# Sliding-window attention feeding a squared-ReLU MLP: the first two token blocks as one unit, w_in in five pieces, a new order

## The chip, the cores and the metric

The kernel runs on one core of a Trainium2 chip. The metric is device time in microseconds (us), the median of several executions. A core has TensorE (PE, matrix products; its weight loads are shown as PEld), VectorE (DVE), ScalarE (ACT), GpSimd (POOL) and SyncE (SP). Transfers are issued from the queues of POOL, SP and ACT, and 16 DMA engines carry them.

## The reference

```python
scores = scale * q @ k.T             # 8 batches, 8 heads, 576 positions, head size 64
bias = slopes * -abs(rel)            # ALiBi: one slope for each head
scores = where(0 <= rel < 128, scores + bias, -1e9)
attn = softmax(scores)               # in float32
x = (attn @ v) -> [4608, 512]        # heads side by side, tokens of all batches in a row
h = x @ w_in                         # [512, 2048]
g = maximum(h, 0) ** 2
out = g @ w_out                      # [2048, 512], float32
```

The window is 128 positions, so a block of 128 queries meets its own block of keys and the one before it.

## The kernel before, in words

**Tiling.** The 576 positions of a batch are four blocks of 128 and one of 64. There are 40 blocks, m = 0 to 39. The first eight are the first blocks of the eight batches (kind "diag", with no block before them); then come the other blocks, two batches at a time. The MLP works on nine groups g of 512 tokens.

**Attention of one block.** POOL loads k, q and v by DMA and casts them to bf16 (lines 408 and 413; block 0's k and q come over SP and ACT as float32, line 391, and DVE casts them). k and q are then transposed: for m < 8 on PE (`tp`, line 464, with copies `ev` by ACT or DVE), for the others by a DMA transpose from SP (`kqT`, line 450). Scores go into four PSUM banks with the tag "a" (`s`, line 520); ACT exponentiates them (`e`, line 544), DVE multiplies by a mask with bias and window in it (`m`, lines 552 to 559). PE multiplies by v in two halves of four heads (`pv`, line 587); v has a column of ones, which gives the sum. DVE takes the reciprocal (`r`, line 605) and normalises (`n`, line 609). The result is transposed into `xT`: on PE for m < 8 (`xp`, line 629, and a copy `x`), by a DMA transpose from SP for the others (`x`, line 617).

**MLP.** For groups 0 to 2 the first product is cut into units: `u g.r.e` (line 721) takes token range r and some of the 16 column blocks (fc) of w_in, always 512 columns of PSUM in a bank with the tag "h" (two of them). In group 0 a unit is 128 tokens by four fc, in groups 1 and 2 it is 256 tokens by two. From group 3 on, one step `fc g.fc` (line 739) takes 512 tokens by one fc. ACT applies ReLU (line 692), DVE squares into `g` (line 683). `o g.t.p` (line 766) multiplies quarter p of the 2048 values by w_out for token block t; after the fourth part ACT or DVE copies it out (`oe`) and SP stores it (`st`, line 790).

**What sets the order.** The kernel writes its own order. Every piece of work is a task with engines, an estimated length, dependencies, buffers and a key (a due time). `Plan.order` (lines 98 to 188) walks an estimated clock: on each engine it takes, of the tasks that can start within NEAR of the earliest, the one with the lowest key. LAND, `lat` and `dma` estimate when a transfer lands; LEAD says how far ahead of its first unit an attention block is due; the table ADJ shifts keys of single tasks by hand. On the chip these estimates only matter by the order that comes out of them; semaphores do the waiting. Where the plan sees a hole on PE in the first 30 us, `fill` (line 269) puts in matmuls on a tile of zeros that compute nothing. Eight more run at the start (line 434).

**Queues.** POOL's first transfers are set by the list FIRST: "b2" is block 2's k, q, v, "i1" a piece of w_in, "o1" a quarter of w_out. POOL keeps at most eight of its transfers under way: the ninth waits for the first to land. SP's queue is in order. Four buffers hold k and q (`kq`), nine hold v, three hold x. The transposes and stores that touch the prediction stand on SP as `st0.2.0 kqT10 st0.3.0 kqT11 x8 kqT12 x9 kqT13 kqT14 st1.0.0 x10`.

**Names in the change.** N_CUT is the number of first blocks whose transpose back (`xp`) is cut into two; N_PVH the number of first jobs whose `pv` uses an "h" bank instead of an "a" bank; N_HW the number of blocks loaded over SP and ACT. A unit waits for its piece of w_in (`t_win`) and for x of all its blocks (`t_x`).

Of the kernel before, what the change touches and what calls it, by code (L numbers as in the profile page):

```python
# [9 lines left out]
BF16 = mybir.dt.bfloat16  # L10
# [2 lines left out]

FIRST = ["b0", "b1", "b2", "i0", "i1", "o0", "i2", "b3", "i3", "o1", "o2", "o3", "b4", "b5", "b6", "b7"]
DIAG = [[0], [1], [2], [3], [4, 5], [6, 7]]
N_HW = 1
N_PE = 8
N_CUT = 2  # L20
N_PVH = 1
N_WARM = 8
FILL = 0.7
LEAD = 1160
IOTA = 3
TP, XP = "h", "h"
UNITS = {0: 128, 1: 256, 2: 256}
CUT = 384
SIZE = {"kq": 4, "v": 9, "kqT": 7, "P": 3, "x": 3}
DUE = {m: 200.0 * m - 1e5 for m in range(40)}  # L30

ADJ = {
    "e1.1": 9000135.6, "e19.2": -177.01, "e19.3": -468.76, "e2.1": 100084.3, "m2.0": 690.7, "m6.1": 98674.82,
    "mask0.6": 99479.82, "n6.1": 98853.62, "o0.1.2": -273.16, "o0.2.1": 39, "o0.3.2": -120.75, "o1.1.0": -108.3,
    "o1.2.3": -99095.7, "o1.3.1": -36.0, "o1.3.2": -98248.6, "o1.3.3": -224.85, "o2.0.0": -99746.7, "o2.0.1": -614.83,
    "o2.0.2": -99764.0, "o2.0.3": -321.48, "o2.2.1": -99007.0, "o2.3.0": -99983.4, "o2.3.1": -875.31,
    "pv0.1": 99179.79, "pv17.0": -148.06, "r0.1": 582.3, "reluu0.0.1": -99432.0, "reluu0.2.2": -9000091.1,
    "reluu0.2.3": -99589.6, "reluu1.0.0": -99692.3, "reluu2.1.2": -52.84, "s13": 168.43, "s17": -99446.52,
    "s20": 342.83, "squ0.1.0": 48, "squ0.2.3": 99864.0, "u0.1.0": -79.4, "u0.1.1": -99420.7, "u0.2.1": -99696.3,
    "u0.2.3": -98883.7, "u1.0.1": -98012.9, "u1.1.3": -99531.7, "u1.1.5": 191.7, "u1.1.6": -410.31,  # L40
    "u2.0.4": -100055.4, "u2.0.5": -342.1, "u2.0.6": -100078.7, "u2.0.7": -331.83, "u2.1.1": 78.7, "u2.1.2": 63.7,
    "u2.1.3": -99113.3, "u2.1.4": -79.4, "u2.1.7": -303.48,
}


def FUSED(g, u):
    return False


class Task:  # L50
# [20 lines left out]
class Plan:  # L71
# [2 lines left out]
    LAT = {"PE": 210.0, "ACT": 60.0, "DVE": 80.0, "POOL": 200.0, "SP": 200.0, "ACTQ": 200.0}  # L74
    BEGIN = {"POOL": 840.0, "SP": 740.0, "ACTQ": 740.0, "ACT": 2550.0, "DVE": 860.0, "PE": 1190.0}
    FIRST = {"POOL": 1100.0, "SP": 1150.0, "ACTQ": 1150.0}
    LAND = {"POOL": 1200.0, "SP": 2200.0, "ACTQ": 900.0}
    TO_SP = 600.0
    LANES = 8
    NEAR = {"PE": 60, "ACT": 0, "DVE": 25}  # L80
    FILL_UNTIL = 30000.0

    def __init__(self, bufs):
# [108 lines left out]
def kernel(  # L192
    ctx: ExitStack, tc: tile.TileContext, q, k, v, moe_w_in, moe_w_out, out
):
    nc = tc.nc
# [78 lines left out]
    def act(n):  # L274
        return n * 0.95 + 115.0
# [4 lines left out]
    def dve_p(n, rate=1):  # L280
        return n / rate / 0.96 + 185.0
# [65 lines left out]
    t_zero = plan.add({"DVE": 1300.0}, -1e5 + 950, zero, name="zero", later=25000.0)  # L347


    t_win = [None] * 4  # L350
    t_wout = [None] * 4

    def load_w(which, n, key):
        def emit():
            w = d_ff // 4
            if which == "in":
                nc.gpsimd.dma_start(w_in_sb[:, :, n * w:(n + 1) * w],  # L357
                                    moe_w_in[:, n * w:(n + 1) * w].rearrange("(c p) f -> p c f", p=128))
            else:
                nc.gpsimd.dma_start(w_out_sb[:, 4 * n:4 * n + 4, :],  # L360
                                    moe_w_out[n * w:(n + 1) * w, :].rearrange("(c p) f -> p c f", p=128))
        t = plan.add({"POOL": 780.0}, key, emit, dma=2600.0, name=f"w_{which}{n}")
        (t_win if which == "in" else t_wout)[n] = t

    s_kq, s_v, t_kq, t_v = {}, {}, {}, {}

# [7 lines left out]
    def load_block(m, key):  # L374
# [10 lines left out]
        if split:  # L385
            stage = stages[m]
            t_l = []
            for i, src in enumerate((k, q)):
                for r, (eng, e) in enumerate((("SP", nc.sync), ("ACTQ", nc.scalar))):
                    def fetch(i=i, src=src, r=r, e=e):  # L390
                        e.dma_start(view(stage, i)[:, r], source(src, m, split)[:, :, r])
                    t_l.append(plan.add({eng: 740.0}, key + 0.1 * i, fetch, dma=330.0, lat=1000.0,
                                        name=f"l{'kq'[i]}{m}.{r}"))

            def cast_kq(i):
                w = slice(i * d_model, (i + 1) * d_model)
                copy((c_k, c_q)[i],
                     kq[s_kq[m].idx][:, w].rearrange("s (i r d) -> s r i d", i=4, d=D),
                     stage[:, w].rearrange("s (r i d) -> s r i d", r=2, d=D))
            engs = {"DVE": 480.0, "ACT": 600.0} if m else {"DVE": 480.0}  # L400
            c_q = None
            c_k = plan.add(engs, key, lambda: cast_kq(0), t_l[0:2], [s_kq[m]], name=f"ck{m}")
            c_q = plan.add(engs, key, lambda: cast_kq(1), t_l[2:4] + [c_k], name=f"cq{m}")
            t_kq[m] = [c_k, c_q]
        else:
            def fetch_kq():
                for i, src in enumerate((k, q)):
                    nc.gpsimd.dma_start(view(kq[s_kq[m].idx], i), source(src, m, split))  # L408
            t_kq[m] = [plan.add({"POOL": 1780.0}, key, fetch_kq, [], [s_kq[m]], dma=2 * ns,
                                name=f"lkq{m}", count=2)]  # L410
# [229 lines left out]


    def ups(g):
        if UP[g] == 512:
            return [("fc", g, u) for u in range(16)]
        return [("unit", g, r, e) for r in range(512 // UP[g]) for e in range(16 * UP[g] // 512)]

    UP = {g: UNITS.get(g, 512) for g in range(NG)}
    work_list = ups(0)
    for g in range(NG):
        up = ups(g + 1) if g + 1 < NG else []  # L650
# [1 line left out]
            work_list += up[u:u + 1] + [("o", g, u // 4, u % 4)]  # L652

    def span_of(item):
        w = UP[item[1]]
        lo = item[1] * 512 + (item[2] * w if w < 512 else 0)
        return lo, lo + w

    def blocks(lo, hi):
        return [at[x] for r in range(lo // 128, hi // 128) for x in ranges[r]]  # L660
# [10 lines left out]

    g_slots, g_sq, g_first, o_slots = {}, {}, {}, {}

    def relu_square(g, slot, last_mm, key, out_of, fused):
        def square(a, b=None):
            if g_slots[g].tile is None:
                g_slots[g].tile = work.tile([128, FCB, 512], BF16, tag="g", bufs=2, name="g")
            o = out_of(g_slots[g].tile)
            i = a if len(o.shape) == 2 else a.rearrange("p (f t) -> p f t", f=o.shape[1])
            if fused:  # L680
                nc.vector.scalar_tensor_tensor(o, i, 0.0, i, op0=ALU.max, op1=ALU.mult)
            else:
                nc.vector.tensor_tensor(o, i, i, op=ALU.mult)  # L683
        if fused:
            ts = plan.add({"DVE": dve_p(512)}, key, lambda: square(slot.tile), [last_mm] + g_sq[g][:1], [], [slot],
                          name=f"rs{g}")
        else:
            srt = Slot("rt")

            def relu():  # L690
                srt.tile = work.tile([128, 512], BF16, tag="rt", bufs=3, name="rt")
                nc.scalar.activation(srt.tile, slot.tile, AF.Relu, bias=0.0, scale=1.0)  # L692
            tr = plan.add({"ACT": act(512)}, key, relu, [last_mm], [srt], [slot], name=f"relu{last_mm.name}")
            ts = plan.add({"DVE": dve(512, 2)}, key, lambda: square(srt.tile), [tr] + g_sq[g][:1], [], [srt],
                          name=f"sq{last_mm.name}")
        g_sq[g].append(ts)
        return ts

    def group(g):
        if g not in g_slots:  # L700
# [1 line left out]
            return [g_slots[g]]  # L702
        return []

    sq_of = {}

    def unit(g, r, e, key):

        new = group(g)
        slot = Slot("h")  # L710
        w = UP[g]
        nf = 512 // w
        lo = g * 512 + r * w
        ms = blocks(lo, lo + w)

        def emit():
            fill(t_mm, bank_of(slot, "h"))
            for f in range(nf):
                fc = nf * e + f
                for cc in range(C):  # L720
                    nc.tensor.matmul(slot.tile[:, f * w:(f + 1) * w], w_in_sb[:, cc, fc * 128:(fc + 1) * 128],  # L721
                                     xT[:, cc, lo:lo + w], start=cc == 0, stop=cc == C - 1)
        t_mm = plan.add({"PE": 4 * nf * mm(w)}, key, emit,
                        [t_win[nf * e // 4], g_first.get(g)] + [x for m in ms for x in t_x[m]], [slot] + new,
                        name=f"u{g}.{r}.{e}")
        g_first.setdefault(g, t_mm)
        ts = relu_square(g, slot, t_mm, key,
                         lambda gt: gt[:, nf * e:nf * e + nf, r * w:(r + 1) * w], FUSED(g, e + r))
        for t in range(r * w // 128, (r + 1) * w // 128):
            sq_of.setdefault((g, t, nf * e // 4), []).append(ts)  # L730

    def fc_step(g, fc, key):
# [3 lines left out]
        def emit():  # L736
            bank(slot, "h")
            for cc in range(C):
                nc.tensor.matmul(slot.tile, w_in_sb[:, cc, fc * 128:(fc + 1) * 128],  # L739
                                 xT[:, cc, g * 512:(g + 1) * 512], start=cc == 0, stop=cc == C - 1)  # L740
        t = plan.add({"PE": 4 * mm(512)}, key, emit,
                     [t_win[fc // 4], g_first.get(g)] + [x for m in blocks(g * 512, g * 512 + 512) for x in t_x[m]],
                     [slot] + new, name=f"fc{g}.{fc}")
        g_first.setdefault(g, t)
        ts = relu_square(g, slot, t, key, lambda gt: gt[:, fc, :], FUSED(g, fc))
        for r in range(4):
            sq_of.setdefault((g, r, fc // 4), []).append(ts)

# [84 lines left out]
```

## Time and profile before

| | |
|---|---|
| median of 3 runs | 316.77 us (316.46 to 316.91) |
| the profiled execution | 316.23 us |
| its span | 314.4 us |
| mean granted PE clock | 0.994 |
| PE busy | 306.3 us (97%), 2794 matmuls |
| DVE, ACT, POOL busy | 174.1, 170.7, 105.5 us |
| POOL's DMA queue: packets' time | 84.5% of 16 engines' span |
| fill and warm-up matmuls | 50 of 128 columns, 8 of 512 |

The span is the time from the first to the last instruction in the profile. Around it lie 1.83 us in that execution. Busy matmul times overlap each other slightly, so a group's busy time is more than what it takes on the path; the view of the chain gives the latter. The granted clock is the share of full speed at which PE was let run. "Idle before, releaser" names what ended a wait. A transfer's time to landing is counted from its issue.

### The profile page before, as it was taken

How to read it: one execution, taken by the hardware profiler on the slowest of the kernel's cores; microseconds unless marked ns; L12 is line 12 of the kernel's file. 1: busy time of each engine (PE TensorE's matmuls, PEld its weight loads, DVE VectorE, ACT ScalarE, POOL GpSimd, SP SyncE). 2: the span in 40 equal slices, each digit the busy share in tenths (PEclk: the TensorE clock that was granted, in tenths of full speed). 3: DMA queues.
4: the chain of work that ended last, by engine and by line, in shares of the span. 5: the costliest groups of instructions: out<-in, count | busy, mean ns of one | idle time of the engine just before them, and what ended most of it. 6: DMA issues, size and time to landing. Idle time of an engine off the chain costs nothing.

```text
span 314.4 us, 7113 instructions
## 1 busy us (share of the span) xinstructions
PE 306.3 (97%) x2794; PEld 176.0 (56%) x2794; DVE 174.1 (55%) x498; ACT 170.7 (54%) x331; POOL 105.5 (34%) x131
## 2 busy tenths in 40 slices
PE   8789999999999999999999999999999999999996
PEld 4679756776766755454554555545554444444443
DVE  3756467766566666776766666666666222222211
ACT  4646436657657625776576655576464443434400
POOL 8826598352622666320966301800000000000000
PEclk9979999999999999999999999999999999999999
DMA  9999999999999999994999999992221100010022
GB/s 134 181 190 206 171 184 163 160 153 171 187 138 138 162 189 167 181 143 95 127 196 170 180 107 122 191 161 83 52 63 23 67 35 34 34 35 33 33 93 76
DMA packets 165714, 39.54 MB, mean 126 GB/s; under 512 B 156336, under 2 KB 161200, under 8 KB 165680
## 3 DMA queue, kind: packets, MB, share of 16 engines
q0 software_dynamic: 114656, 18.10, 84.5%
q1 hardware_dynamic: 50592, 20.65, 34.9%
q8 instruction: 22, 0.36, 0.5%
q10 hardware_dynamic: 432, 0.33, 0.3%
q14 instruction: 12, 0.10, 0.1%
HBM read 36.70 MB, written 9.44 MB: 147 GB/s over the span
## 4 chain that ended last, share of the span: by engine, by line
PE 92%; DMA 5%; POOL 2%; issue 0%; ACT 0%; POOLq 0%
PE o L766 39%; PE h L739 27%; PE h L721 14%; PE pv L587 6%; PE s L520 5%; DMA w_in_sb<-in_moe_w_in_dram 3%; DMA xT<-x 2%; POOL kq L408 1%; POOL vf L413 1%; PE tp L464 1%; PE xp L629 0%; POOL w_in_sb L357 0%; POOL dist L304 0%; ACT osb L290 0%; POOLq L304 0%
## 5 line engine op out<-in xcount | busy, mean ns | idle before, releaser
L766 PE MATMUL o<-w_out_sb,g 128*128 128x512 bf16 (+2 forms) x592 | 142.4, 373 | 0.0
L692 ACT ACTIVATE rt<-h 128x512 bf16<-128x512 f32 x144 | 85.8, 609 | 91.4 <-PE h L739 63.3
L683 DVE TENSOR_TENSOR g<-rt 128x512 bf16<-128x512 bf16 x144 | 60.3, 422 | 66.8 <-ACT rt L692 66.0
L739 PE MATMUL h<-xT,w_in_sb 128*128 128x512 bf16 x384 | 96.1, 379 | 0.0
L766 PEld LDWEIGHTS <-g 128*128 128x128 bf16 x592 | 54.5, 98 | 56.5
L544 ACT ACTIVATE P<-s 128x512 bf16<-128x512 f32 (+1 forms) x136 | 67.2, 582 | 17.3 <-PE s L520 17.3
L739 PEld LDWEIGHTS <-w_in_sb 128*128 128x128 bf16 x384 | 34.6, 98 | 38.2
L552 DVE TENSOR_TENSOR P<-P,masks 128x512 bf16<-128x512 bf16 (+1 forms) x112 | 44.6, 405 | 14.7 <-ACT P L544 9.8
L721 PE MATMUL h<-xT,w_in_sb 128*128 128x128 bf16 (+1 forms) x512 | 47.9, 250 | 3.0 <-DMA w_in_sb<-in_moe_w_in_dram 2.3
L408 POOL DMA_DIRECT2D kq<-in_k_dram x39 | 33.4, 856 | 36.4 <-DMA kqT<-kq 26.9
L721 PEld LDWEIGHTS <-w_in_sb 128*128 128x128 bf16 x512 | 39.7, 100 | 8.7 <-DMA w_in_sb<-in_moe_w_in_dram 2.7
L413 POOL DMA_DIRECT2D vt<-in_v_dram x32 | 27.2, 855 | 46.2 <-PE pv L587 43.7
L408 POOL DMA_DIRECT2D kq<-in_q_dram x39 | 33.5, 860 | 8.3 <-DMA kq<-in_q_dram 2.4
L609 DVE TENSOR_TENSOR x<-pv,rec 128x256 bf16<-128x256 f32 (+1 forms) x80 | 33.8, 423 | 2.7
L587 PEld LDWEIGHTS <-P 128*128 128x128 bf16 (+1 forms) x576 | 25.6, 101 | 14.1 <-DVE P L559 1.7
L290 ACT ACTIVATE osb<-o 128x512 f32<-128x512 f32 (+1 forms) x24 | 14.2, 590 | 23.4 <-PE o L766 23.4
L605 DVE RECIPROCAL rec<-pv 128x4 f32<-128x4 f32 (+1 forms) x80 | 14.2, 178 | 22.7 <-PE pv L587 20.2
L587 PE MATMUL pv<-vt,P 128*128 128x65 bf16 (+1 forms) x448 | 24.0, 194 | 0.0
L288 DVE COPY osb<-o 128x512 f32<-128x512 f32 (+1 forms) x13 | 8.9, 681 | 15.1 <-PE o L766 14.6
L520 PEld LDWEIGHTS <-kqT 64*128 64x128 bf16 x448 | 12.4, 94 | 7.6 <-issue 7.2
L520 PE MATMUL s<-kqT 64*128 64x128 bf16 (+1 forms) x256 | 15.6, 210 | 0.0
L520 PE MATMUL s<-kqT,kqT 64*128 64x128 bf16 (+1 forms) x192 | 11.4, 210 | 0.0
(40 smaller groups left out, 96.3 us busy)
## 6 DMA issues: line engine op xcount, KB each, us to landing
out_dram<-osb SPq DMA_DIRECT2D x31, 256.0 KB, 5.1
kq<-in_k_dram POOLq DMA_DIRECT2D x31, 128.0 KB, 6.9
kq<-in_q_dram POOLq DMA_DIRECT2D x31, 128.0 KB, 7.6
vt<-in_v_dram POOLq DMA_DIRECT2D x24, 128.0 KB, 7.6
w_in_sb<-in_moe_w_in_dram POOLq DMA_DIRECT2D x4, 512.0 KB, 10.9
w_out_sb<-in_moe_w_out_dram POOLq DMA_DIRECT2D x4, 512.0 KB, 15.0
vf<-in_v_dram POOLq DMA_DIRECT2D x8, 128.0 KB, 6.2
out_dram<-osb SPq DMA_DIRECT2D x8, 128.0 KB, 2.4
```

What stands on the lines that cost most here:

```text
L408: nc.gpsimd.dma_start(view(kq[s_kq[m].idx], i), source(src, m, split))
L413: nc.gpsimd.dma_start(tile_of(s_v[m])[0:n, :, 0:D], source(v, m))
L520: nc.tensor.matmul(sS[2 * g2 + r].tile[:, jj * 256 + c0:jj * 256 + c0 + w], tile_of(s_kqT[mk])[rows, c, :], tile_of(s_kqT[mq])[rows, C + c ...
L544: nc.scalar.activation(flat(Pt[sP.idx]), sS[i].tile.rearrange("p (j t) -> p j t", j=2)[:, :, lo:hi], AF.Exp, bias=0.0, scale=scale)
L552: nc.vector.tensor_tensor(flat(Pt[sP.idx]), flat(Pt[sP.idx]), flat(masks), op=ALU.mult)
L587: nc.tensor.matmul(sv.tile[0:n, hi * (D + 1):(hi + 1) * (D + 1)], Pt[sP.idx][:, place(h)].rearrange("p t q -> p (t q)")[:, w], tile_of(s_v ...
L609: nc.vector.tensor_tensor(xt[sx.idx][0:n, hf * 256:(hf + 1) * 256].rearrange("p (h e) -> p h e", h=4), heads(sv)[0:n, :, 0:D], sr.tile[0:n ...
L683: nc.vector.tensor_tensor(o, i, i, op=ALU.mult)
L692: nc.scalar.activation(srt.tile, slot.tile, AF.Relu, bias=0.0, scale=1.0)
L721: nc.tensor.matmul(slot.tile[:, f * w:(f + 1) * w], w_in_sb[:, cc, fc * 128:(fc + 1) * 128], xT[:, cc, lo:lo + w], start=cc == 0, stop=cc ...
L739: nc.tensor.matmul(slot.tile, w_in_sb[:, cc, fc * 128:(fc + 1) * 128], xT[:, cc, g * 512:(g + 1) * 512], start=cc == 0, stop=cc == C - 1)
L766: nc.tensor.matmul(slot.tile[:, 0:hi - lo], gt[:, fc, t * 128:(t + 1) * 128], w_out_sb[:, fc, lo:hi], start=fc == 0, stop=fc == FCB - 1)
```

## The change

Group 0 has a table of token ranges: 256 tokens by two fc, then twice 128 tokens by four fc. w_in is loaded in five pieces of 2, 2, 4, 4, 4 column blocks (two eighths and three quarters) instead of four quarters; each unit waits for the pieces that hold its own column blocks. In the list FIRST the two eighths come ahead of block 2, and the next two pieces ahead of the first quarter of w_out. N_CUT goes from 2 to 1, N_PVH from 1 to 0. LAND, `lat`, `dma`, NEAR and LEAD, which only the planner reads, and the table ADJ are changed. The option of fusing ReLU and square, which was never taken, is removed.

```diff
-FIRST = ["b0", "b1", "b2", "i0", "i1", "o0", "i2", "b3", "i3", "o1", "o2", "o3", "b4", "b5", "b6", "b7"]
+FIRST = ["b0", "b1", "i0", "i1", "b2", "i2", "i3", "o0", "b3", "i4", "o1", "o2", "o3", "b4", "b5", "b6", "b7"]
-N_CUT = 2
-N_PVH = 1
+N_CUT = 1
+N_PVH = 0
-LEAD = 1160
+LEAD = 2000
-UNITS = {0: 128, 1: 256, 2: 256}
+UNITS = {0: [(0, 256, 2), (256, 128, 4), (384, 128, 4)], 1: [(0, 256, 2), (256, 256, 2)],
+         2: [(0, 256, 2), (256, 256, 2)]}
+PIECES = [2, 2, 4, 4, 4]
...
 ADJ = {
...
-    LAND = {"POOL": 1200.0, "SP": 2200.0, "ACTQ": 900.0}
+    LAND = {"POOL": 2400.0, "SP": 2200.0, "ACTQ": 900.0}
-    NEAR = {"PE": 60, "ACT": 0, "DVE": 25}
+    NEAR = {"PE": 25, "ACT": 0, "DVE": 0}
...
     def load_w(which, n, key):
+        lo, hi = (sum(PIECES[:n]), sum(PIECES[:n + 1])) if which == "in" else (4 * n, 4 * n + 4)
+
         def emit():
             w = d_ff // 4
             if which == "in":
-                nc.gpsimd.dma_start(w_in_sb[:, :, n * w:(n + 1) * w],
-                                    moe_w_in[:, n * w:(n + 1) * w].rearrange("(c p) f -> p c f", p=128))
+                nc.gpsimd.dma_start(w_in_sb[:, :, lo * 128:hi * 128],
+                                    moe_w_in[:, lo * 128:hi * 128].rearrange("(c p) f -> p c f", p=128))
...
-        t = plan.add({"POOL": 780.0}, key, emit, dma=2600.0, name=f"w_{which}{n}")
-        (t_win if which == "in" else t_wout)[n] = t
+        t = plan.add({"POOL": 780.0}, key, emit, dma=650.0 * (hi - lo), lat=2900.0, name=f"w_{which}{n}")
+        if which == "in":
+            t_win[lo:hi] = [t] * (hi - lo)
+        else:
+            t_wout[n] = t
...
-                for r, (eng, e) in enumerate((("SP", nc.sync), ("ACTQ", nc.scalar))):
+                for r, (eng, e) in enumerate((("SP", nc.sync), ("SP", nc.sync) if m else ("ACTQ", nc.scalar))):
...
-                    t_l.append(plan.add({eng: 740.0}, key + 0.1 * i, fetch, dma=330.0, lat=1000.0,
+                    t_l.append(plan.add({eng: 740.0}, key + 0.1 * i, fetch, dma=330.0, lat=700.0 if i else 1650.0,
...
-        w = UP[g]
-        nf = 512 // w
-        lo = g * 512 + r * w
+        at_r, w, nf = UNITS[g][r]
+        lo = g * 512 + at_r
...
-                        [t_win[nf * e // 4], g_first.get(g)] + [x for m in ms for x in t_x[m]], [slot] + new,
+                        t_win[nf * e:nf * e + nf] + [g_first.get(g)] + [x for m in ms for x in t_x[m]], [slot] + new,
```

The order that comes out, on PE up to the fourth piece of w_in (in brackets the fill matmuls ahead of a task):

```
before: warm tp0.0 tp0.1(9) s0.0(9) tp1.0 s0.1 tp1.1 pv0.0(7) s1(5) tp2.0 xp0.0 tp2.1 pv0.1 s2(14) pv1.0
        xp0.1(6) pv1.1 xp1.0 u0.0.0 xp1.1 u0.1.1 pv2.0 pv2.1 u0.1.0 u0.0.1 xp2.0 o0.0.0 u0.2.1 u0.0.2
        u0.1.2 tp3.0 o0.1.0 tp3.1 u0.2.0
after:  warm tp0.0 tp0.1(4) s0.0(9) s0.1(2) pv0.0(9) tp1.0 tp1.1 pv0.1 xp0.0(6) xp0.1(6) s1 pv1.0(18)
        pv1.1(5) tp2.0 tp2.1 xp1.0 s2(2) u0.0.0 u0.0.1 pv2.0 u0.0.2 u0.0.3 pv2.1 u0.0.4(8) xp2.0 u0.0.5
        u0.1.2 u0.1.1 tp3.0 o0.1.0 tp3.1 o0.0.0 s3 u0.1.0 u0.0.6
```

Around the start of group 2 the order on PE is `u1.1.5 s11 o1.2.0 o1.2.1 u2.0.0 u2.0.6 u2.0.4` before, and `u1.1.5 o1.1.2 pv10.1 o1.2.0 o1.1.3 s11 o1.2.1 o1.2.2 u2.0.0 pv11.0 u2.0.1` after. SP's order after is `st0.1.0 st0.0.0 st0.3.0 kqT8 kqT9 st0.2.0 kqT10 kqT11 x8 kqT12 x9 st1.0.0 kqT13 kqT14 x10`.

## Prediction

> **What bounds the kernel now.** I began with the busy shares: PE 306.3 of 314.4 us (97%), DVE 55%, ACT 54%. A change can only win where PE stands still, runs at a lower clock, or does work that computes nothing. The windows of 5 us say where that is (span, then busy time of PE, PEld, DVE, ACT, POOL, then granted clock, DMA share, GB/s):
>
> ```profile
> 5.00:10.00 5.00, 4.88 (x67) 4.12 (x66) 2.96 (x10) 2.75 (x9) 5.00 (x8) 1.00 2.31 147
> 10.00:15.00 5.00, 3.19 (x55) 2.54 (x55) 4.00 (x21) 3.47 (x11) 4.11 (x5) 1.00 1.33 192
> 15.00:20.00 5.00, 3.60 (x45) 3.43 (x46) 1.17 (x5) 1.11 (x2) 1.49 (x2) 0.72 1.24 205
> 20.00:25.00 5.00, 5.00 (x75) 4.53 (x74) 3.34 (x19) 3.47 (x13) 2.24 (x3) 0.94 1.85 181
> ```
>
> PE loses 1.8 us in 10 to 15, 1.4 us in 15 to 20, and part of its clock until 25. From 20 us on the waits of PE name one thing only, the second line here; the first is the start:
>
> ```profile
> PE h L721 <- DMA w_in_sb<-in_moe_w_in_dram: 2.3, 2, 1.4
> ...
> PE h L721 <- DMA xT<-x: 0.7, 1, 0.7
> ```
>
> The chain of work that ended last passes through a DMA at the same two places (start, length):
>
> ```profile
> 8.45 9.07 DMA w_in_sb<-in_moe_w_in_dram
> ...
> 74.45 6.03 DMA xT<-x
> ```
>
> So PE is bound by its own work except at transfers. I then followed the transfers. The issues view, asked in narrow windows, gives each landing (the last number is us from issue):
>
> ```profile
> w_in_sb<-in_moe_w_in_dram POOLq DMA_DIRECT2D x1, 512.0 KB, 7.2
> ...
> w_in_sb<-in_moe_w_in_dram POOLq DMA_DIRECT2D x1, 512.0 KB, 14.5
> ...
> kq<-in_q_dram POOLq DMA_DIRECT2D x1, 128.0 KB, 11.1
> ```
>
> Issue plus landing time, from POOL's timeline: k1 6.8 us, q1 8.1, v1 8.9, k2 9.8, q2 10.7, v2 11.5, first w_in quarter 14.9, second 17.5, first w_out 20.1, third w_in 22.6, k3 23.4, q3 24.3, v3 25.6, fourth w_in 13.25 + 14.5 = 27.8, then w_out 30.2, 32.8, 35.3. Read the spacing: 0.87 us for a k, q or v, about 2.55 us for a weight quarter, with no hole from 5 us on. POOL's DMA queue is one pipe that never runs dry here; order changes who lands when, not when the pipe is through. It is still full much later:
>
> ```profile
> 61.98 0.87 POOL L408 DMA_DIRECT2D kq<-in_q_dram  x1 [2.42 <-DMA kq<-in_q_dram]
> ...
> 73.12 1.23 SPq L450 DMA_TRANSPOSE kqT<-kq  x1
> 74.45 1.29 SPq L617 DMA_TRANSPOSE xT<-x  x1
> ```
> ```profile
> 80.52 2.79 PE L721 MATMUL h<-xT,w_in_sb 128*128 128x256 bf16 x24 [0.65 <-DMA xT<-x]
> ```
>
> q12 lands at 61.98 + 11.1 = 73.1; SP's in-order queue holds kqT12 until then, and behind it x9, which lands at 74.45 + 6.03 = 80.5. PE had been waiting for it 0.65 us. After this PE never waits again until the tail. This gate, not the first 20 us alone, decides what a better start is worth.
>
> **The change, part by part.**
>
> *Pieces and order of w_in.* Queue now: b0 b1 i0 i1 (eighths) b2 i2 i3 o0 b3 i4. A quarter writes 512 runs of 1 KB (32 for each of 16 engines: 2.55 us / 32 = 80 ns a run); a k writes 1024 runs of 128 B (64 each: 13.6 ns). An eighth has 512 runs of 512 B; a line through the two rows gives 42 ns, 32 x 42 = 1.35 us. Two eighths cost 2.70 against 2.55: everything behind them +0.15 us. Bounds: 1.28 us each if only bytes count (+0), 2.55 if only runs count (+2.55). The byte-like end is nearer, since runs eight times larger take six times as long. [...] The extra issue is some 0.8 us on POOL, hidden: later POOL issues wait for landings anyway. Landings then: eighths 10.3 to 11.0 and 11.6 to 12.4, k2 12.6, q2 13.5, v2 14.4, i2 16.9 to 17.6, i3 19.5 to 20.1, o0 22.7, k3 23.5, i4 28.0 (ranges, because the first weight in the old trace landed 0.8 later than the spacing says).
>
> *Unit of 256 tokens.* It needs both x0 and x1. 128 matmuls of 128 columns become 64 of 256: the chain has 3.57 us / 64 = 55.8 ns and 1.75 / 16 = 109 ns, so 128 x 55.8 - 64 x 109 = 0.14 us less on PE. ReLU and square stay 16 x 512 columns for the group, at 0.60 and 0.42 us.
>
> *Block 1.* N_CUT and N_PVH put pv0 into the scores' banks, so s1 waits for n0.1 (behind s1: its exponentials, masks, pv1, x1), and block 2's k and q land 2.8 us later with s2, tp2 and, by the new order, xp1 behind them. Chaining the old intervals: tp0.1 0.5 us earlier (4 fill matmuls instead of 9), n0.1 ends 10.1, s1 10.4 (9.4 before), exponentials to 11.9, n1.1 ends 13.5, tp2.1 at q2's landing 13.6, xp1 13.8, its copy to 14.8. First unit at 15.0, as before (14.99). If q2 is 0.5 us later, so is this.
>
> *PE from there.* u0.0.0, u0.0.1 to 16.75 (0.875 each); 17.3 i2: two units to 19.1; 19.9 i3: two, with pv2 and xp2, to 21.9; u0.1.2, u0.1.1 (0.89 each) to 23.7; tp3, two o of 0.86, s3, u0.1.0 to 27.1; then idle to i4, 28.0. At 28.0 the new kernel has done one unit and s3 more than the old one at 27.9: 0.89 + 0.3 - 0.1 = 1.1 us ahead. The idle 0.9 us before i4 forgives that much lateness earlier.
>
> *The clock.* Shortfall 5 x 0.28 + 5 x 0.06 = 1.7 us: PE at half clock for 3.4 us, from 17.4. [...] I take no fall; if it falls, PE reaches i4 at 28.4 to 28.9 instead of 28.0, up to 0.9 us of the lead.
>
> *The gate at 80.5.* Comparing the orders of PE up to u2.0.0, the new one does the same work plus one o (o1.2.2, 0.86 us). PE would arrive at 79.87 - 1.1 + 0.86 = 79.6. x9 is still behind kqT12 on SP (kqT11, x8, kqT12, x9), q12 has the same bytes before it; the store of o0.3 moves ahead of kqT8, which is not short (s8 comes 2 us after kqT8 lands). So x9 lands at 80.5 + 0.15 = 80.65: PE waits 1.0 us and gets out 0.15 us later with 0.86 us less to do: **-0.71 us**. The rest of the gain at the start is given back here.
>
> *After the gate* (LEAD 2000, NEAR, ADJ: order only, no instruction added). Attention comes earlier. The tightest edge I find is x11 to u2.1.4: x11 lands about 91, the unit comes about 92.3. Cover 1.3 us; when it is gone, lost one for one. Fill matmuls, 69 for 50, lie in waits. The ACTQ branch does nothing while N_HW is 1. Tail unchanged.
>
> Sum: span 314.4 - 0.71 = 313.7; with the 1.83 us around it (316.23 - 314.4) 315.5. The median shown is 0.54 above that execution, so 316.77 - 0.71 = **316.06 us**, -0.22%. Under 0.2% (0.63 us) this kernel's measurement can hardly be told from no change.
>
> **Rivals.**
> - *Gate opens early.* Transposes and transfers share engines, and the rate drops around 53, 60 and 70 us; if x9 lands by 79.6, the start's 1.1 plus the old 0.65 us of wait all come through: 316.77 - 1.75 + 0.15 = 315.2. Against: the same bytes.
> - *Hidden anyway.* The gate moves by 0.4 to 1.3 us, or the x11 edge takes as much: 316.2 to 317.2, say 316.7. Here the eighths do nothing that lasts.
> - [...]
> - *It doesn't do what it says:* first unit not earlier. That is in my main line already (15.0); the gain is density after it.
>
> **How the numbers follow.** Main line 0.46 (316.06, own range 315.6 to 316.5: above 316.4 it counts as no change), gate early 0.11 (315.2), hidden 0.22 (316.7), slower 0.21 (317.9; half of it beyond 317.9). Faster: 0.40 of the main and all of the early case, 0.51; same: 0.06 + 0.22 less 0.01, 0.27; slower 0.22. The range leaves out half of the early case's low side and the far half of the slow one: 315.0 to 317.9.
>
> **What would show it.** Right: eighths landing near 11 and 12.4; first h matmul at 15.0, and of 256 columns; clock 1.00 from 15 to 25; a wait for w_in near 27 to 28; a PE wait for xT at 80 to 81, longer than 0.65 (about 1.0), as the only one from 30 us on. Wrong: x9 landing off 80.5 by more than 0.5, a second wait of PE after 81, or i4 later than 28.5.

## The result and the profile after

The changed kernel takes **314.45 us** (median of 4, 314.08 to 314.79), the kernel before 316.76 us beside it (316.46 to 316.91): a ratio of 0.9928, 95% interval 0.9911 to 0.9945. That is 2.3 us less; forecast were 0.7 less (316.06), with a range from 315.0 to 317.9. The profiled executions differ by 1.6 us, in time (316.23 and 314.6 us) as in span (314.4 and 312.8).

The start went as worked out, all but the length of one wait. The windows of 5 us of the kernel after (columns as before: span, busy PE, PEld, DVE, ACT, POOL, granted clock, DMA share, GB/s), and its waits of PE:

```profile
10.00:15.00 5.00, 4.22 (x76) 3.55 (x73) 4.03 (x20) 2.77 (x8) 5.00 (x7) 1.00 1.88 180
15.00:20.00 5.00, 4.93 (x59) 4.39 (x54) 3.79 (x16) 4.26 (x14) 1.54 (x3) 1.00 1.24 205
20.00:25.00 5.00, 4.58 (x56) 3.76 (x56) 2.47 (x16) 4.03 (x9) 2.41 (x4) 1.00 1.86 180
```
```profile
PE tp L470 <- DVE kq L289: 1.2, 1, 1.2
PE h L718 <- DMA w_in_sb<-in_moe_w_in_dram: 0.4, 1, 0.4
```

The clock is 1.00 throughout, and of the 2.3 us of waiting for w_in 0.4 is left, where the last piece of w_in lands. But there is no wait for xT at all: the gate at 80.5, on which the forecast rested, stood open. The timelines of PE and of SP's queue:

```profile
15.20 1.91 PE L718 MATMUL h<-xT,w_in_sb 128*128 128x256 bf16 x16
...
28.03 1.05 PE L718 MATMUL h<-xT,w_in_sb 128*128 128x256 bf16 x8 [0.43 <-DMA w_in_sb<-in_moe_w_in_dram]
...
79.75 1.04 PE L718 MATMUL h<-xT,w_in_sb 128*128 128x256 bf16 x8
```
```profile
71.94 1.28 SPq L456 DMA_TRANSPOSE kqT<-kq  x1
73.31 1.30 SPq L623 DMA_TRANSPOSE xT<-x  x1
```

PE reaches the first unit of group 2 at 79.75, foreseen at 79.6. x9 is issued at 73.31 and, by the issues view, takes 6.0 us as before: it lands at 79.3 and not at 80.65. kqT12, ahead of it on SP, goes out at 71.94 instead of 73.12. So the 1.6 us of span are 0.77 (79.75 against 80.52) plus the unit of output work of 0.86 us that PE has done by then in addition. What has to be explained is why the transposes ran 1.2 us earlier. One thing ahead of them is not as it was: x8's transpose is issued at 67.49 instead of 63.72, and lands behind q12 instead of ahead of it.

### The profile page after: what moved, and what is told of

It reads as the page before. It is cut to its first block, busy times and chain, and to the rows that moved or that the text cites. A ratio compares the mean times of both kernels' runs of the same rounds, so it can differ in the third digit from the quotient of the medians.

```text
span 312.8 us, 6974 instructions
## 1 busy us (share of the span) xinstructions
PE 302.5 (97%) x2707; PEld 174.3 (56%) x2749; DVE 172.2 (55%) x494; ACT 172.3 (55%) x334; POOL 106.3 (34%) x132
## 4 chain that ended last, share of the span: by engine, by line
PE 85%; DMA 7%; POOL 5%; issue 2%; ACT 1%; DVE 0%; POOLq 0%
PE o L762 37%; PE h L735 26%; PE h L718 11%; PE pv L593 6%; PE s L526 5%; DMA w_in_sb<-in_moe_w_in_dram 5%; DMA kq<-in_k_dram 2%; POOL kq L414 2%; POOL vf L419 1%; POOL w_in_sb L360 1%; ACT P L550 0%; PE xp L635 0%; POOL w_out_sb L363 0%; PE tp L470 0%; ACT rt L683 0%
## 5 line engine op out<-in xcount | busy, mean ns | idle before, releaser
L762 PE MATMUL o<-w_out_sb,g 128*128 128x512 bf16 (+2 forms) x560 | 137.6, 373 | 2.5 <-issue 1.3
L762 PEld LDWEIGHTS <-g 128*128 128x128 bf16 x592 | 53.3, 98 | 54.1
L735 PEld LDWEIGHTS <-w_in_sb 128*128 128x128 bf16 x384 | 35.7, 98 | 40.0
L718 PE MATMUL h<-xT,w_in_sb 128*128 128x256 bf16 (+1 forms) x448 | 47.0, 257 | 0.9 <-DMA w_in_sb<-in_moe_w_in_dram 0.4
L718 PEld LDWEIGHTS <-w_in_sb 128*128 128x128 bf16 x448 | 37.2, 98 | 7.0 <-DMA w_in_sb<-in_moe_w_in_dram 0.6
L291 ACT ACTIVATE osb<-o 128x512 f32<-128x512 f32 (+1 forms) x23 | 13.4, 583 | 24.3 <-PE o L762 23.0
L611 DVE RECIPROCAL rec<-pv 128x4 f32<-128x4 f32 (+1 forms) x80 | 14.3, 179 | 17.6 <-PE pv L593 15.3
```

The lines of the kernel that those rows point to most:

```text
L762: nc.tensor.matmul(slot.tile[:, 0:hi - lo], gt[:, fc, t * 128:(t + 1) * 128], w_out_sb[:, fc, lo:hi], start=fc == 0, stop=fc == FCB - 1)
```

## The experiments

All kernels that change an order replay it from a written list instead of planning it, so that nothing moves but what is named. Each time is a median of 5 to 12 executions (of before again there is one), next to executions of the kernel before on the same chip (medians there 316.85 to 317.19, single ones from 315.8 to 321.4).

**First round: which part of the change earns the time.** Before's profile was taken once more, and the order was cut at the first unit of group 1 (u1.0.0): the start of one kernel with the rest of the other. A fourth kernel is before with x9 ahead of kqT12 on SP.

> The kernel before, unchanged, to see how far its wait for x9 varies. Gate theory (the waits of PE are set by DMA landings, above all x9): the one wait of PE after 30 us is again for xT near 80 us; if the typical execution is slower than the one profiled (316.23 against a median of 316.76), this wait is 0.65 to 1.3 us here. Rival (the difference lies elsewhere): the wait is 0.65 again whatever the time.

> The changed kernel up to u1.0.0, and from there on the order of the kernel before, on all engines (block 8's scores and values early again, o1.2.2 after u2.0.0). Gate theory: x8's transpose is again ahead of q12 in the DMA engines, x9 lands at 80.3 to 80.9 as before, PE comes some 1.1 us earlier and waits for it 1.3 to 1.9 us; the whole of the start is given back: 316.3 to 317.0, ratio 0.999 to 1.001. Rival (the start is what was gained, the gate was chance): wait gone or as before, 315.0 to 315.7, ratio 0.994 to 0.997.

> The kernel before up to u1.0.0, and from there on the order of the changed kernel. Gate theory: block 8 late, x8's transpose behind q12, x9 lands near 79.3; PE has o1.2.2 more to do before it, reaches u2.0.0 near 80.7 and doesn't wait: 0.65 us less, more where the typical wait is longer: 315.5 to 316.2, ratio 0.996 to 0.998. Rival (the start is what was gained): 316.5 to 316.9, ratio 0.999 to 1.0005.

> The kernel before with one step moved: x9's transpose ahead of kqT12's in SP's queue. Gate theory: x9 no longer stands behind q12's landing, is issued near 70 us and lands near 76; the wait of 0.65 us at 80.5 is gone and nothing else waits (s12 needs kqT12 only near 86): 315.5 to 316.2, ratio 0.996 to 0.998. Rival (something else holds PE there, or the next wait takes it back): 316.5 to 316.9, ratio 0.999 to 1.0005.

```diff
# start only: after's order up to u1.0.0, before's behind it; rest only: the other way round
# x9 first, in before's SP order
-kqT11 x8 kqT12 x9
+kqT11 x8 x9 kqT12
```

Measured: before again 317.12 us (span 315.3); start only 314.95, ratio 0.9919 (0.9887 to 0.9951); rest only 316.26, 0.9963 (0.9929 to 0.9998); x9 first 315.34, 0.9948 (0.9926 to 0.9970). Two waits for x9 were not as foreseen: 0.4 us in before again (0.65 to 1.3) and 0.6 us in rest only (none). It looked as if the start alone brought the gain. Yet its kqT12 goes out at 72.09, with before's order of transfers behind the start, and in the other three kernels at 72.9 or later.

What differs is seen in the DMA view of narrow windows (first row the busy share in 40 slices, here of 0.05 us; then the rate; then queues with packets, MB and share). The kernel before, from 68 to 70 us and from 78 to 80:

```profile
DMA  9999999999999999999999999901000100110111
GB/s 151 166 159 154 156 164 156 151 497 138 141 148 156 138 151 166 143 143 149 143 167 128 123 64 28 13 0 8 8 8 8 8 8 8 10 13 8 10 13 8
...
q8 instruction: 1, 0.02, 3.0%
```
```profile
GB/s 297 297 282 236 51 389 191 282 251 282 266 271 276 261 287 123 41 31 0 0 0 0 0 0 0 0 0 5 5 5 5 10 10 10 10 10 10 10 10 10
...
q8 instruction: 1, 0.02, 3.5%
```

The kernel after, from 68 to 70, and from 71 to 73, where its packet is:

```profile
GB/s 148 172 154 148 164 161 159 161 161 148 151 169 156 156 161 172 146 148 164 159 159 161 169 151 146 169 154 166 151 174 146 149 164 164 154 166 161 146 139 122
```
```profile
GB/s 154 154 149 164 156 159 159 161 148 156 156 149 159 144 469 146 146 154 138 146 143 154 141 156 146 151 146 159 133 151 166 143 143 151 164 146 149 166 161 161
...
q8 instruction: 1, 0.02, 3.0%
```

In before all 16 DMA engines fall from 150 or 280 GB/s to 13 and less, from 69.2 for 0.9 us and from 78.9 for 1.3 us (both run on past the windows shown), each time 0.6 to 0.8 us behind the start of one packet of the queue named instruction (the slices of 497 and 389 GB/s are these packets). The first hole lies ahead of q12's landing, the second in x9's own flight. After has a packet at 71.7, behind which the rate stays at 150 for 1.5 us (then a dip of 0.3 us, at 73.3); its next hole comes past 82, when x9 has landed. That these packets bring the program itself I read from the name of their queue; no trace shows what is in them. The pages count 22 of them in the kernel before, 0.36 MB in all, and 21 after, 0.34 MB: 16 KB each. PE's stream, a weight load and a matmul for each product, has twice 2,794 = 5,588 rows before and twice 2,749 = 5,498 after by the weight loads on the pages: 64 matmuls saved by the wider unit, 19 fill matmuls added, two rows each. That makes 254 rows to a packet before (5,588 / 22) and 262 after (5,498 / 21); the 256 used below is an estimate between the two. So the theory is: **the change moved the packets by 90 rows, some 3.3 us, and out of the transposes that matter.** (The expectations below put these packets some 0.3 us later than the slices do.)

**Second round: only the rows.** The warm-up (8 matmuls of 512 columns on zeros, from 1.2 to 4.7 us) is cut into more and narrower ones of the same columns in sum. It ends within 0.2 us of where it did, and nothing behind it is changed: 45 more matmuls, 90 rows, give after the alignment of before; 83 more, 166 rows, give before that of after (256 less 90). Two further kernels fill PE's two waits for w_in in before with matmuls on zeros, to keep the clock up (it was 0.999 or more in all 11 executions of the first of these, and in 8 of 11 of the second, which has 166 more rows too).

```diff
 def warm_up():
-    for _ in range(N_WARM):          # 8
-        nc.tensor.matmul(s_warm.tile, warm[:, 0:128], warm, start=True, stop=True)
+    for _ in range(53):              # in after; 91 of 45 columns in before
+        nc.tensor.matmul(s_warm.tile[:, 0:77], warm[:, 0:128], warm[:, 0:77], start=True, stop=True)
# clock: in unit(), ahead of the products of u0.0.0 and u0.1.1
+    for _ in range({"u0.0.0": 3, "u0.1.1": 5}.get(t_mm.name, 0)):
+        nc.tensor.matmul(slot.tile, warm[:, 0:128], warm, start=True, stop=True)
```

> The kernel after, with the warm-up as 53 matmuls of 77 columns in place of 8 of 512 (the same columns, 45 more matmuls: 90 more rows in PE's instruction stream). Theory (an instruction packet that falls among DMA transposes stops the pipe for about 1 us, and where it falls goes by the number of PE's instructions ahead of it): the packet that after has at 72.0 us moves some 3.5 us forward, to 67.5 to 69, into the transposes of kqT11 and x8 and ahead of q12; the 2-us DMA view shows there a hole of 0.7 to 1.1 us at 8 to 10 GB/s, kqT12 is issued near 72.9 to 73.3 instead of 71.9, and PE waits 0.4 to 0.9 us for x9 at u2.0.0; 314.9 to 315.4. Rival (the pipe ran early because PE and the issues came earlier, and the packets do not matter): kqT12 at 71.9 to 72.2, no wait for xT, 314.3 to 314.6.

> The kernel before, with the warm-up as 91 matmuls of 45 columns (83 more matmuls, 166 more rows: with packets of 256 rows the same alignment as after, 90 rows fewer). Theory of the packets: packets near 62 and 72 in place of 59, 68.7 and 78.5; no hole between 66 and 71, kqT12 near 72.0 to 72.3 instead of 73.1, and PE's wait of 0.65 us for x9 falls to 0 to 0.2; 315.9 to 316.3 beside a before of 316.8. Rival (PE's pace decides when the pipe is through): kqT12 at 73.0 or later, the wait stays, 316.6 to 316.9.

> The kernel before, with 3 matmuls of 512 columns on zeros ahead of its first unit and 5 ahead of its second, in PE's two waits for w_in (0.93 and 1.40 us). Theory of the clock: the granted clock is 1.00 from 15 to 25 us, PE is ahead by 1.0 to 1.7 us at 28; but x9 is still where it was (kqT12 near 73), so PE only waits longer for it, 1.5 to 2.0 us instead of 0.65, and the time is 316.0 to 316.4, less the spread that the clock brings. Rival (the clock falls for another reason than the waits): 0.7 to 0.95 from 15 to 25 again, 316.8. A second rival (nothing gates at 80): the whole lead comes through, 315.1 to 315.6.

> Both edits in the kernel before: the 8 matmuls in the waits for w_in, and a warm-up of 83 matmuls of 49 columns, which brings the added rows to the same 166. Theories of the packets and the clock together: clock 1.00, no hole between 66 and 71, kqT12 near 72.0, PE waits 0.3 to 1.2 us less for x9 than in the kernel with the clock edit alone; 314.8 to 315.5. If only the clock counts: as the clock edit alone, 316.0 to 316.4. If neither: 316.8.

- **After with 90 more rows: 316.45 us** (315.81 to 317.0, 11 executions), 2.0 more than after; ratio to before 0.9971 (0.9947 to 0.9995). More than foreseen.
- **Before with 166 more rows: 315.48 us**, ratio 0.9941 (0.9906 to 0.9976): 83 matmuls that compute nothing make it 1.5 us faster, more than foreseen.
- Before with the clock kept: 316.32 us, 0.9977 (0.9954 to 0.9999); with clock and rows: 315.76, 0.9961 (0.9927 to 0.9995), a little above what was foreseen.

After with 90 more rows has holes at both places again. Its windows 68 to 70 and 78 to 80, then the waits and the timeline of PE:

```profile
GB/s 481 151 151 148 148 149 123 141 141 133 123 133 141 108 113 82 44 23 5 8 8 8 8 8 8 10 8 13 8 10 10 8 8 10 13 64 166 154 148 169
...
q8 instruction: 1, 0.02, 2.9%
```
```profile
GB/s 159 179 174 169 210 292 282 252 580 271 272 276 266 267 266 271 369 62 56 144 77 36 10 0 0 0 0 0 0 0 5 5 10 5 10 10 10 5 10 10
```
```profile
PE h L847 <- DMA xT<-x: 1.3, 1, 1.3
...
PE h L864 <- DMA xT<-x: 0.8, 1, 0.8
```
```profile
81.14 1.03 PE L847 MATMUL h<-xT,w_in_sb 128*128 128x256 bf16 x8 [1.33 <-DMA xT<-x]
```

x9 was issued at 74.13 and took 6.9 us, to 81.0. PE waits 1.3 us for it, where at most 0.9 was foreseen, and 0.8 us for another xT at 119, where none was (a packet at 112.8 and a hole at 114.2 lie ahead of that); together these are the 2.0 us.

In before with 166 more rows kqT12 did not go out near 72, as foreseen, but at 73.5, and x9 at 74.87, later than in before. But x9 took 4.5 us, to 79.4, with no such hole at 68 to 70 nor here, in its window 78 to 80 (no packet in it; the packet before is at 72.8):

```profile
GB/s 287 292 287 233 292 287 297 287 282 297 282 297 232 67 26 200 287 287 292 297 287 297 261 266 159 202 220 210 182 202 174 166 159 184 154 143 166 164 148 164
```

So the hole that goes with the rows is the second, in x9's own flight. The first does not explain the 1.2 us. The kernel after has a hole ahead of q12's landing too, from 63.0 to 63.8, behind its packet at 61.5. Its window from 63 to 72 (slices of 0.225 us) begins in it:

```profile
GB/s 13 9 10 61 158 158 160 158 139 154 157 155 150 154 148 156 149 156 155 157 161 159 156 160 156 159 160 157 158 158 152 143 156 156 151 154 156 156 220 147
```

And q12's time to landing hardly moves with the rows: 9.7 us in after and 9.9 with 90 more rows, 11.1 us in before and 11.0 with 166 more.

**Third round: a full period, and controls.**

> The kernel after once more, on the chip of this batch. Theory of the packets: packets near 62 and 72 us as in its first profile, kqT12 near 72, no wait for xT at u2.0.0; 314.2 to 314.8. It is the yardstick for the other three. Rival (the early landing of x9 was chance in one execution): a wait for xT of 0.5 us or more, and a time of 315.5 or more.

> The kernel after with the warm-up as 136 matmuls of 30 columns: 128 more matmuls, 256 more rows, one whole packet of 256 rows. Theory of the packets: the alignment is that of after again (packets near 61 and 71 to 72 us, no hole ahead of q12, no wait for xT at u2.0.0); 314.3 to 314.9, though 90 more rows alone cost 2 us. Rival (more matmuls in the warm-up cost by themselves, or more code does): 316.5 or more, slower than with 90 more rows.

> The kernel after with w_in in four quarters again (queue b0, b1, i0, b2, i1, i2, o0, b3, i3), the order of all engines as in after. Theory (the eighths do nothing, since the first unit waits for x1 at 15.0 and a quarter there has landed by 12.4): first unit at 15.0 to 15.2, what is behind it in the queue 0.0 to 0.15 us earlier, 314.2 to 314.8, the same as after. Rival (the eighths are what makes the start early): first unit later than 15.5 and 315.0 or more. [...]

> The kernel after with 90 more rows in the warm-up (the alignment of before, 316.45 us) and x9 issued ahead of kqT12 on SP, so that it does not wait for q12's landing. Theory (the packets cost time only through x9's late landing at u2.0.0 and one later transpose): x9 lands before 79, no wait at u2.0.0, the wait of 0.8 us for xT at 119 may stay; 314.6 to 315.4. Rival (the rows cost elsewhere): 316.2 or more.

```diff
# full period: warm-up of 136 matmuls of 30 columns, 256 more rows
# quarters
-PIECES = [2, 2, 4, 4, 4]
-FIRST = ["b0", "b1", "i0", "i1", "b2", "i2", "i3", "o0", "b3", "i4", ...]
+PIECES = [4, 4, 4, 4]
+FIRST = ["b0", "b1", "i0", "b2", "i1", "i2", "o0", "b3", "i3", ...]
# 90 rows and x9 ahead of kqT12 on SP
```

After again: **314.45 us** (314.26 to 314.95, 5 executions), ratio 0.9886 (0.9836 to 0.9936). With **256 more rows: 314.72** (314.44 to 314.85), though 90 rows cost 2.0: the price is not that of more matmuls or more code, it has the period of a packet. Its packets lie near 62 and 72 again; the rate from 68 to 70 us stays between 138 and 172 GB/s. But kqT12 goes out at 72.7, not near 72, and PE still does not wait for x9.

With quarters 314.70 us (314.06 to 315.97), first unit at 15.33: no difference that these executions can tell from after, so nothing that the eighths gain or cost shows here. The last piece of w_in lands at 27.81 (27.98 in after), and 0.15 us was what the eighths were forecast to cost. With 90 rows and x9 first 316.34 (315.15 to 317.68, and two executions at 320.4): a miss, I had foreseen 314.6 to 315.4. The profiled execution is one of the two longest (span 318.6), so only the place in it is used: x9 is waited for no more, but x11, one unit further, is, for 2.7 us. The queue's order alone does not mend it.

**Fourth round: the missing cells.** With the packets known, the first round had compared unlike things: start only has after's number of rows, rest only before's.

> The start of after (to its last unit of the first group) with before's order behind it, and 90 more rows in the warm-up (53 matmuls of 77 columns), so that PE's stream is as long as before's. Theory (packets cost 1.5 to 2 us, the start gains 0.5 to 1.0 in either alignment): packets near 58, 68 and 78.5, kqT12 near 73, a wait for xT of 0.5 to 1.5 us at u2.0.0; 316.1 to 316.8, against 314.95 without the rows. Rival (only after's order behind the start suffers from the packets): 314.8 to 315.3.

> Before's start with after's order behind it, and 166 more rows in the warm-up (91 matmuls of 45 columns): packets as in after. Theory: packets near 62 and 72, kqT12 near 72 to 73, no wait for xT; 314.9 to 315.6, against 316.26 without the rows, and 0.5 to 1.0 behind after, which is what the start is worth. Rival (rows matter only with after's start): 316.0 to 316.5.

> The kernel after with the warm-up as 31 matmuls of 132 columns, 46 more rows, half the shift: packets near 60, 70.2 and 80. If a packet stops the pipe whenever transposes are in flight: a hole near 70.2, still ahead of q12, kqT12 near 72.8 and a wait for xT of 0.3 to 1.3 us, 315.0 to 316.5. If only a packet in a certain stretch of a transpose does, as the one at 72.0 that cost nothing in after: no hole there, 314.3 to 314.8.

```diff
# start only with the warm-up of 53 matmuls of 77 columns; rest only with that of 91 of 45; after with 31 of 132
```

Start only with 90 more rows: 316.71 us, ratio 0.9998 (0.9966 to 1.0030), but with kqT12 at 72.2, where 73 was foreseen, and a wait for x9 of 0.4 us instead of 0.5 to 1.5. Rest only with 166 more: 314.77, 0.9932 (0.9905 to 0.9960), a little faster than foreseen. After with 46 more rows: 315.17, 0.9947 (0.9917 to 0.9976), between the two ends; its packet at 70.6 makes no hole, one at 80.2 does, and there is no wait for xT at group 2. All eight cells, medians in us ("start, rest" says whose order stands up to u1.0.0, and whose behind it):

| start, rest | packets as in before (5,588 rows) | packets as in after (5,498 or 256 more) | difference |
|---|---|---|---|
| before, before | 316.97 (316.85 to 317.19 by batch) | 315.48 | -1.5 |
| after, before | 316.71 | 314.95 | -1.8 |
| before, after | 316.26 | 314.77 | -1.5 |
| after, after | 316.45 | 314.45 (314.72) | -2.0 (-1.7) |

The right column wins in every row, by more than any single step down the table brings. By the ratios the four differences are 1.9, 2.5, 1.0 and 1.4 to 2.7 us; the intervals of the third pair overlap. Down the columns, start and rest together bring 0.5 us with before's packets and 0.8 to 1.0 with after's; which of the two earns it is within the scatter, all the more as the cells come from four batches.

The traces say where the rows act. One profile for each cell (in brackets before again; after again and after with 256 more rows), packets as in before / as in after:

| start, rest | kqT12 goes out, us | x9's time to landing, us | x9 lands, us |
|---|---|---|---|
| before, before | 73.12 (73.92) / 73.54 | 6.03 (6.06) / 4.55 | 80.48 (81.31) / 79.41 |
| after, before | 72.22 / 72.09 | 6.33 / 4.53 | 79.88 / 78.08 |
| before, after | 72.92 / 72.04 | 5.89 / 5.54 | 80.14 / 78.92 |
| after, after | 72.79 / 71.94 (71.20; 72.67) | 6.88 / 6.00 (5.24; 5.76) | 81.00 / 79.31 (78.47; 79.76) |

With before's packets x9 takes longer in every row and lands later, by 1.1 to 1.8 us without the brackets. When kqT12 goes out does not follow the rows. With before's order behind the start it is early in both alignments with after's start, and late in both with before's; in the lower two rows it is some 0.9 us later with before's packets, but 256 more rows, which give after's alignment, have it at 72.67. Start only, and below it start only with 90 more rows:

```profile
72.09 1.37 SPq L585 DMA_TRANSPOSE kqT<-kq  x1
...
72.22 1.23 SPq L585 DMA_TRANSPOSE kqT<-kq  x1
```

So the early kqT12 of start only, which led to the theory, belongs to the start as far as single profiles tell, and the theory holds for another place than the one it was made for.

## Why the prediction was wrong, point by point

**The step that failed** is the last of the gate: "q12 has the same bytes before it [...] So x9 lands at 80.5 + 0.15 = 80.65: PE waits 1.0 us". It landed at 79.3, and PE did not wait. The landing is not made by bytes alone: in the 80.5 that I took over lay a hole of 1.3 us in x9's own flight, behind an instruction packet. The change took 90 rows out of PE's stream, and I had priced these at 0.14 us of PE's time and nothing else; with nothing but 90 rows put back x9 lands at 81.0. Nor were the bytes ahead of q12 the same, with x8's transpose behind it; q12 landed 1.2 us earlier, which the rows were not found to cause. The view that would have shown the holes was at hand: I noted that "the rate drops around 53, 60 and 70 us" and did not ask what fell into the drop. With the rows put back, the change brings 0.5 us by the medians (316.45 against 316.97) and 0.9 by the ratio, and the forecast was 0.7. That is near, but in part luck: the wait for x9 is then 1.3 us where 1.0 was foreseen, the wait of 0.8 us at 119 had no term at all, and neither had what before loses by its clock (below).

**The rival that came true** is "gate opens early", at 315.2 with a chance of 0.11: x9 landed by 79.6, as it asks. Its size was off by one term: the 0.54 us by which before's median lies above before's profiled execution. I added it to the new kernel too. After's executions lie within 0.7 us, and its median of 314.45 is near its profiled execution: 316.23 - 1.6 = 314.6.

**Right:** first unit at 15.20 (15.0) and 256 columns wide; by issue and landing time the first eighth at 4.98 + 5.5 = 10.5 and the third piece at 9.07 + 7.9 = 17.0 (10.3 to 11.0, and 16.9 to 17.6); the last piece at 28.0 to the tenth, with 0.4 us of idle PE ahead of it where I had 0.9; PE at group 2 at 79.75 (79.6). The 317.9 of the case "slower" holds a price for one transfer more that no run shows: with quarters the last piece of w_in lands 0.17 us earlier than in after (27.81 against 27.98), near the 0.15 that I added. After 81 us no wait appeared; the edge named as the tightest, x11, is the one that breaks in the kernel with 90 rows and x9 first.

**The clock.** "I take no fall" was right: 1.00. It was an estimate: with the waits filled the clock stayed up (below), but how much idle time brings a fall is not shown. (In the first profile of before the half clock, 0.50 granted, lasts from 17.2 to 20.6 us; I had it begin at 17.4.) What before loses by it is less than the shortfall, as the gate takes most of it back. Before again ran at a lower clock than its first profile, for these two windows:

```profile
15.00:20.00 5.00, 3.88 (x42) 3.61 (x43) 0.84 (x3) 0.77 (x2) 1.49 (x2) 0.58 1.24 205
20.00:25.00 5.00, 5.00 (x61) 4.52 (x59) 3.32 (x19) 2.92 (x10) 1.92 (x3) 0.74 1.84 181
```

That is a shortfall of 5 x 0.42 + 5 x 0.26 = 3.4 us, twice that of the first profile; yet its span is only 0.9 us longer. And of before's executions beside the four rounds (102, three near 321 us left out), the 20 with a mean clock of 0.998 or more have a median of 316.5 us, the 79 others 317.0. So it is some 0.5 us. With the waits filled all 11 executions had a clock of 0.999 or more, and 0.65 us of the time went; PE's wait for x9 grew from 0.65 to 1.4 us, foreseen for the clock theory as 1.5 to 2.0:

```profile
81.16 1.05 PE L853 MATMUL h<-xT,w_in_sb 128*128 128x256 bf16 x8 [1.35 <-DMA xT<-x]
```

**What stays open.** That the time and x9's landing go with the rows is shown by rows alone, in four pairs, and for the time over one period. That they do so through the packets and holes is seen in the traces; how one packet of 16 KB stops 16 engines is not shown. Nor is it fully shown when: those at 71.7 in after and at 70.6 with 46 rows fell among transfers too, and cost nothing. There nearly all of these came from POOL's queue (1,841 of 2,118 DMA packets from 71 to 73 us in after, 2,324 of 2,362 from 70 to 72 with 46 rows). Counted over the 17 traces from 30 to 125 us, 43 of 69 packets that start while SP's queue (transposes and stores) moves 60 GB/s or more are followed within 2 us by half a microsecond under 30 GB/s, and 2 of 35 that start while it moves less than 1. Packets are not the only cause of such holes: 40 of 98 have none in the 2 us before, as that at 80.4 in start only. A shallower dip, 13 to 60 GB/s for up to 0.8 us, lies near 76 to 77.5 in most kernels of both columns with no packet in it; its cause was not looked for. Why q12 lands 1.2 us earlier in after is open too: the start and x8's later transpose are both candidates. And x9's time to landing is 6.0 us in after as in before, though the hole is gone; it may be that the store st1.0.0, now ahead of kqT13, slows it, which no run tests.

## What to carry to other kernels

Where a kernel hangs on DMA transposes, a change of a few dozen PE instructions can move the instruction packets and with them up to 2 us (here 90 rows: 3.3 us, and 2.0 us of the time), more than the change itself may be worth: put a like number of rows back (a warm-up cut finer does it; 256 more rows left after within 0.3 us), and compare at equal alignment before an edit is credited. When a landing time is carried over from one kernel to the next, look for holes in the rate, ahead of it and in its own flight, and name what is in them. If nothing else is to be had, the alignment itself is a knob: 83 empty matmuls were worth 1.5 us to the kernel before; no kernel here beat the changed one.

## What was unexpected in the hardware

- One instruction packet, of 22 that take 0.5% of the DMA engines' time in all, can be followed by 0.8 to 1.3 us in which the 16 engines together move 0 to 15 GB/s instead of 150 to 290, when transposes are under way.
- The clock at the start is not a property of the program: the same kernel had 0.72 and 0.94 in the windows from 15 and 20 us in one execution, 0.58 and 0.74 in another, and before with 166 more rows, with waits of 0.6 and 1.4 us for w_in, had 1.00 in both. In the two executions with the lower clock PE's longest wait for w_in was of 1.4 and 1.5 us, against the 1.4 of the third. So a wait of that length comes with either clock, and what decides between the two is not shown.
